# W_O's first row loaded by 16 transfers of 15, 14, ... 1 and 8 partitions

## The chip, the cores and the metric

The kernel runs on one core of a Trainium2 chip. The metric is the device time of one execution in microseconds; times of several executions are given as a median. One core has five engines with instruction streams of their own: TensorE (PE in the profile, with its weight loads as PEld), VectorE (DVE), ScalarE (ACT), GpSimd (POOL) and SyncE (SP), which here only issues transfers and waits. Its 16 DMA engines move the bytes; a transfer that is issued is cut over several of them, and they work through what is queued in order.

## The reference, cut to what matters

One decode step of a parallel block: attention over the last 4096 cached positions and a gated feed-forward layer, both fed from the same normalised input, and both added to it.

```python
xn = layernorm(x)                                  # x: 4 x 1 x 512
q = (xn @ wq) as 32 heads of 128
k, v = last 4096 positions of k_cache, v_cache     # 8 heads of keys and values
o = softmax(q k^T / sqrt(128)) v                   # 4 query heads share one of keys and values
attn = o @ wo                                      # wo: 4096 x 512
ffn = (silu(xn @ w_gate) * (xn @ w_up)) @ w_down
out = x + attn + ffn
```

All tensors are bf16. The four sequences, eight key-value heads, 4096 positions and 128 columns make 64 MiB of K and V in all; the weights are another 13 MiB, of which W_O is 4 MiB.

## The kernel before

The order of everything is written out by hand, one stream per engine, with semaphores between them. All transfers of weights, K and V are issued by SyncE, in one order: W_Q, W_gate, W_up, then for each of the eight key-value heads K in two halves and V (with W_down behind the first V), then W_O, then half of the output. K and V have one buffer each. A half of K for the next head is issued when TensorE has transposed that half of the head before (`load_k` waits on `s_tr`), V when the head before has gone through its second product (`load_v` waits on `s_pv`). W_O has a buffer of its own, and its loads wait for nothing but their turn behind the last V.

A head's loop on TensorE (L487 to L506): 16 chunks of K are transposed into PSUM (L414), copied out by VectorE and ScalarE (L330, L283), and multiplied with the queries (L427). The maxima are reduced and fed back (L434, L439), ScalarE takes the exponentials (L286), and the product with V is accumulated along with the denominators (L450, L455). Matmuls whose result nobody reads (`spin`, L467) stand in some of the waits.

After the last head comes the tail. TensorE multiplies the gated activations with W_down (L473, 14 matmuls), finishes the last head's sums (L462, L463) and permutes the attention output (L513); VectorE scales it (L353 to L358) and puts it into `OP` (L374). Then W_O: its 4096 rows are held as `WO`, 128 partitions by `NR` = 32 rows of 512 columns, so that partition p holds rows 32p to 32p + 31. In the text, a row of W_O is one of these 32: 1 KB on each of 128 partitions, 128 KB in all. The rows come in four loads, cut at `WOS`:

```python
WOS = (0, 22, 27, 30, 32)
def load_wo(n, a, b):
    eng.dma_start(WO[:, a:b, :], wo_ap[:, a:b, :]).then_inc(d_wo[n], 16)
```

For each load q TensorE waits on `d_wo[q]` and then multiplies its rows (L517 to L528). Rows 0 to 21 go four at a time into one PSUM tile (`acc4`, L473). When they are done, ScalarE copies this tile to `S2` (L294). Rows 22 to 26 go straight into the output's tile (`acc`, L477, four matmuls for each row); then TensorE waits for the copy, sums its four parts with a selection matrix (L477 with `sel4` and `S2`), and takes rows 27 to 29 and 30 to 31. VectorE adds x (L377), and SyncE and ScalarE store the output in four transfers (L268, L297).

Of the kernel before, what the change touches and what calls it, by code (L numbers as in the profile page):

```python
# [10 lines left out]
def bass_parallel_sum__sliding_block_cached__swiglu_ffn__decode_kernel(  # L11
# [10 lines left out]
    out: bass.AP,  # L22
):
    B, _, D = A_x.shape
    _, HKV, Sk, Dh = A_k_cache.shape
    HQ = A_wq.shape[1] // Dh
    F = B_w_gate.shape[1]
# [18 lines left out]
    OFF = -1.0e9  # L46
    WOS = (0, 22, 27, 30, 32)
    WOE = 22
    NR = HQ * Dh // 128

    def sb(name, shape, dtype, align=32):
        return nc.alloc_sbuf_tensor(name, shape, dtype, align_bytes=align)
# [5 lines left out]
    WD = sb("wd_sb", [128, NF, D], BF16, 512)  # L58
    WO = sb("wo_sb", [128, NR, D], BF16, 512)
    X = sb("x_sb", [B, D], BF16, 512)  # L60
# [24 lines left out]

    OP = sb("oP", [128, NR, 32], BF16)
    X4 = sb("x4", [128, D // 4], BF16)
# [12 lines left out]
    dq = sb("dq", [128, 4], FP32)  # L100
    dr = sb("dr", [128, NR], BF16)
    sel = sb("sel", [128, 32], FP32)
# [20 lines left out]
    acc4_ps = ps_S[1]  # L123
    perm_ps = ps_kt[2][:, 0:B * NR]

    def sem(name):
        return nc.alloc_semaphore(name=name)
# [7 lines left out]
    d_wo = [sem("d_wo%d" % q) for q in range(4)]  # L135
    d_k = [sem("d_k%d" % s) for s in range(2)]
    d_v = sem("d_v")
    s_const = sem("s_const")
    s_zero = sem("s_zero")
    s_var = sem("s_var")  # L140
# [34 lines left out]
    wd_ap = B_w_down.rearrange("(p t) n -> p t n", t=NF)  # L175
    wo_ap = A_wo.rearrange("(p r) n -> p r n", r=NR)

    def kv_ap(cache, g, a, b):
        return cache[:, g, Sk - W:, :].rearrange("b (j t) d -> j b t d", j=NJ)[:, :, a:b, :]

    with nc.Block() as block:

        @block.gpsimd
        def _(eng):
# [19 lines left out]
            def select(t, pattern, op, fill, base, mult):  # L204
                eng.affine_select(t, t, pattern=pattern, compare_op=op, fill=fill, base=base,
                                  channel_multiplier=mult)
# [9 lines left out]
            select(dq[:], [[-32, 4]], ALU.is_ge, 0.0, 0, 1)  # L216
            select(dr[:], [[-1, NR]], ALU.not_equal, 1.0, 0, 1)
            eng.drain()
# [19 lines left out]
        @block.sync  # L238
        def _(eng):
            H = NT // 2  # L240

            def load_k(g, h):
                if g > 0:
                    eng.wait_ge(s_tr, NCH * (g - 1) + (h + 1) * NCH // 2)
                eng.dma_start(KB[:, h * H:(h + 1) * H, :], kv_ap(A_k_cache, g, h * H, (h + 1) * H)).then_inc(d_k[h], 16)

            def load_v(g):
                if g > 0:
                    eng.wait_ge(s_pv, g)
                eng.dma_start(VB[:], kv_ap(A_v_cache, g, 0, NT)).then_inc(d_v, 16)  # L250

            def load_wo(n, a, b):
                eng.dma_start(WO[:, a:b, :], wo_ap[:, a:b, :]).then_inc(d_wo[n], 16)

            eng.dma_start(WQ[:], wq_ap).then_inc(d_wq, 16)
            eng.dma_start(WG[:], wg_ap).then_inc(d_wg, 16)
            eng.dma_start(WU[:], wu_ap).then_inc(d_wu, 16)
            for g in range(HKV):
                load_k(g, 0)
                load_k(g, 1)  # L260
                load_v(g)
                if g == 0:
                    eng.dma_start(WD[:], wd_ap).then_inc(d_wd, 16)
            for q in range(4):
                load_wo(q, WOS[q], WOS[q + 1])
            eng.wait_ge(s_y, 1)
            for n in range(2):
                eng.dma_start(out_ap[n], y[32 * n:32 * n + B, :]).then_inc(d_out, 16)  # L268
            eng.wait_ge(d_out, 64)
# [110 lines left out]
        def _(eng):  # L380
# [91 lines left out]
            def acc4(n, left, right, start, stop):  # L472
                return mm(acc4_ps[32 * n:32 * n + 32, :], left, right, start=start, stop=stop, skip_group_check=True)  # L473

            def acc(left, right, start, stop):
                for n in range(4):
                    last = mm(acc_ps[32 * n:32 * n + B, :], left, right[:, HD * n:HD * (n + 1)],  # L477
                              start=start, stop=stop, skip_group_check=True)
                return last
# [36 lines left out]
            eng.wait_ge(s_pc, 1)  # L516
            for q in range(4):  # L517
                eng.wait_ge(d_wo[q], 16)
                for e in range(WOS[q], WOS[q + 1]):
                    if e < WOE:  # L520
                        last = acc4(e % 4, OP[:, e, :], WO[:, e, :], False, e >= WOE - 4)
                    else:
                        last = acc(OP[:, e, 0:B], WO[:, e, :], e == WOE, e == NR - 1)
                if WOS[q + 1] == WOE:
                    last.then_inc(s_e, 1)
                if q == 1:
                    eng.wait_ge(s_ec, 1)
                    acc(sel4[:], S2[:], False, False)  # L528
# [29 lines left out]
```

## Time and profile before

| | us |
|---|---|
| median of 3 runs | 196.94 (196.72 to 197.49) |
| the profiled execution | 196.62 |
| its span, first to last instruction | 194.9 |
| PE busy | 160.3 (82%) |
| DVE busy | 101.7 (52%) |
| ACT busy | 61.1 (31%) |
| HBM read | 81.01 MB, 416 GB/s over the span |

The profile is that of one execution. Its page gives busy time of each engine, a digit or a rate for each fortieth of the span, and the chain that ended last, followed back from the last instruction to what released each step. Other views give the same execution in more detail: the chain in order of time, a timeline of instructions, the issues of transfers with the time from issue to landing, the instructions of one source line, and the busy time and DMA rate in stretches that one chooses. A row of the timeline reads: start, duration, engine, line, operation, written tile <- read tiles, shape, count. The engine SPq is SyncE's queue of issues; the duration there is that of issuing, not of moving. In the row of a stretch, x counts the instructions that touch it.

### The profile page before, as it was taken

Reading aid. Unit: us, or ns where it says so; the run is one execution under the profiler, and the core shown is the slowest. Engines: PE = TensorE matmul, PEld = TensorE weight load, DVE = VectorE, ACT = ScalarE, POOL = GpSimd, SP = SyncE. Lnnn points to the kernel's source line nnn. Section 1 sums busy time; section 2 is a strip of 40 time slices with the busy share of each in tenths; the row PEclk is TensorE's granted clock in tenths of the full one; section 3 lists DMA queues with packets and bytes.
Section 4 is the critical chain, followed back from the end, with each engine's and each line's share of the span. In section 5 each row is a group of like instructions: output and inputs, shape, how many; then the busy total and the mean of one; then the engine's idle time right before and its main releaser. Section 6 shows DMA issues by size and latency. Waiting matters only on the chain.

```text
span 194.9 us, 8285 instructions
## 1 busy us (share of the span) xinstructions
PE 160.3 (82%) x3646; PEld 131.6 (68%) x3646; DVE 101.7 (52%) x217; ACT 61.1 (31%) x77; POOL 12.0 (6%) x51
## 2 busy tenths in 40 slices
PE   0137759958699979997999799979997999799984
PEld 0127759946698569856985597559756976697632
DVE  4200025870478348824882588258825882588230
ACT  2020002524064406440634063407340734073401
POOL 8870000000000000000000000000000000000000
PEclk9999999985999999999999999999999999999999
DMA  6999999999999999999999999999999999999991
GB/s 216 430 435 430 418 427 437 434 424 423 427 481 425 387 430 474 430 397 430 464 430 414 430 454 430 414 430 447 437 420 430 441 430 420 430 441 430 436 396 67
DMA packets 4688, 81.13 MB, mean 416 GB/s; under 512 B 580, under 2 KB 584, under 8 KB 968
## 3 DMA queue, kind: packets, MB, share of 16 engines
q1 hardware_dynamic: 4624, 81.01, 97.2%
q8 instruction: 6, 0.10, 0.2%
q10 hardware_dynamic: 56, 0.01, 0.0%
q14 instruction: 2, 0.02, 0.0%
HBM read 81.01 MB, written 0.00 MB: 416 GB/s over the span
## 4 chain that ended last, share of the span: by engine, by line
DMA 63%; PE 32%; DVE 2%; issue 1%; ACT 0%; SPq 0%; DVEq 0%
DMA kbuf<-in_A_k_cache_dram 52%; PE ps_kt L414 18%; DMA wu_sb<-in_B_w_up_dram 11%; PE ps_s L427 5%; PE ps_o L399 2%; PE ps_kt L467 2%; PE ps_s L473 1%; PE ps_o L463 1%; PE ps_o L450 1%; PE ps_o L462 1%; DVE kT L330 1%; PE ps_s L439 0%; PE ps_s L477 0%; DVE oP L374 0%; ACT s L294 0%
## 5 line engine op out<-in xcount | busy, mean ns | idle before, releaser
L414 PE MATMUL ps_kt<-ident,kbuf 128*128 128x128 bf16 x1024 | 76.5, 221 | 10.2 <-DMA kbuf<-in_A_k_cache_dram 8.2
L330 DVE COPY kT<-ps_kt 128x1024 bf16<-128x1024 bf16 x88 | 57.6, 686 | 21.6 <-PE ps_kt L414 21.6
L414 PEld LDWEIGHTS ps_kt<-ident,kbuf 128*128 128x128 bf16 x1024 | 59.2, 98 | 13.4 <-DMA kbuf<-in_A_k_cache_dram 13.4
L283 ACT ACTIVATE kT<-ps_kt 128x1024 bf16<-128x1024 bf16 x40 | 41.0, 1024 | 65.5 <-PE ps_kt L414 65.5
L427 PE MATMUL ps_s<-qC,kT 128*128 128x16 bf16 x1024 | 44.6, 170 | 3.1 <-DVE kT L330 2.1
L427 PEld LDWEIGHTS ps_s<-qC,kT 128*128 128x128 bf16 x1024 | 37.5, 97 | 4.6 <-DVE kT L330 4.1
L286 ACT ACTIVATE p<-ps_s 128x512 bf16<-128x512 f32 x32 | 16.5, 602 | 34.7 <-PE ps_s L439 34.7
L467 PE MATMUL ps_kt<-own,ones 128*128 128x512 bf16 x102 | 25.9, 380 | 0.0
L336 DVE TENSOR_REDUCE mx<-ps_s 128x16 f32<-128x512 f32 x32 | 22.0, 689 | 5.7 <-PE ps_s L427 3.6
L450 PEld LDWEIGHTS ps_o<-vbuf,p 128*32 128x32 bf16 x1024 | 17.8, 102 | 4.6 <-ACT p L286 4.6
L450 PE MATMUL ps_o<-vbuf,p 128*32 128x128 bf16 x1024 | 19.2, 228 | 0.3
L348 DVE COPY osb<-ps_o 128x128 f32<-128x128 f32 x8 | 2.3, 292 | 29.9 <-PE ps_o L455 29.9
L455 PE MATMUL ps_o<-p,ones 128*32 128x256 bf16 x64 | 17.0, 287 | 0.0
L467 PEld LDWEIGHTS ps_kt<-own,ones 128*128 128x128 bf16 x102 | 8.2, 98 | 8.2 <-issue 1.1
L439 PE MATMUL ps_s<-cm,own 128*128 128x512 bf16 x32 | 9.1, 411 | 1.0 <-DVE cm L345 1.0
L385 PE MATMUL ps_s<-i,xn 4*128 4x4 f32 x4 | 0.6, 261 | 9.2 <-POOLq L226 9.2
L385 PEld LDWEIGHTS ps_s<-i,xn 4*128 4x128 f32 x4 | 0.6, 206 | 9.2 <-POOLq L226 9.2
L455 PEld LDWEIGHTS ps_o<-p,ones 128*32 128x32 bf16 x64 | 6.5, 101 | 0.0
L439 PEld LDWEIGHTS ps_s<-cm,own 128*128 128x128 bf16 x32 | 2.6, 101 | 5.7 <-DVE cm L345 3.5
L392 PE MATMUL ps_s<-xnT,wq_sb 128*128 128x4 bf16 x128 | 3.6, 166 | 3.4 <-DMA wq_sb<-in_A_wq_dram 3.4
L392 PEld LDWEIGHTS ps_s<-xnT,wq_sb 128*128 128x128 bf16 x128 | 3.5, 104 | 3.5 <-issue 3.5
L362 DVE TENSOR_SCALAR ex<-ex 128x56 f32<-128x56 f32 x1 | 0.2, 192 | 9.1 <-ACT ex L290 9.1
(84 smaller groups left out, 77.4 us busy)
## 6 DMA issues: line engine op xcount, KB each, us to landing
kbuf<-in_A_k_cache_dram SPq DMA_DIRECT2D x16, 2048.0 KB, 14.1
vbuf<-in_A_v_cache_dram SPq DMA_DIRECT2D x8, 4096.0 KB, 16.5
wq_sb<-in_A_wq_dram SPq DMA_DIRECT2D x1, 4096.0 KB, 12.3
wo_sb<-in_A_wo_dram SPq DMA_DIRECT2D x1, 2816.0 KB, 22.6
wg_sb<-in_B_w_gate_dram SPq DMA_DIRECT2D x1, 1792.0 KB, 16.7
wu_sb<-in_B_w_up_dram SPq DMA_DIRECT2D x1, 1792.0 KB, 20.9
wd_sb<-in_B_w_down_dram SPq DMA_DIRECT2D x1, 1792.0 KB, 42.1
wo_sb<-in_A_wo_dram SPq DMA_DIRECT2D x1, 640.0 KB, 23.5
```

The lines of the kernel that those rows point to most:

```text
L283: eng.activation(KT[:, c % 4], kt_ps[c % 3], ACT.Copy).then_inc(s_ea, 1)
L286: eng.activation(P[:, BT * q:BT * (q + 1), :], ps_S[q][:].rearrange("p (t n) -> p t n", n=NH), ACT.Exp, scale=SCALE).then_inc(s_p, 1)
L330: eng.tensor_copy(KT[:, c % 4], kt_ps[c % 3]).then_inc(s_ev, 1)
L336: eng.tensor_reduce(mx[:, q, :], ps_S[q][:].rearrange("p (t n) -> p n t", n=NH), AX.X, ALU.max)
L392: last = mm(q_ps[:, h * B:(h + 1) * B], WQ[:, c, h * Dh:(h + 1) * Dh], XnT[:, c, :], start=(c == 0 and h == 0), stop=(c == NC - 1), skip_g ...
L399: last = mm(o[:, t * B:(t + 1) * B], w[:].rearrange("p c (m t) -> p c t m", t=NF)[:, c, t, :], XnT[:, c, :], start=(w is WG and t == 0 and ...
L414: last = eng.transpose(kt_ps[c % 3][:, k, :], KB[:, CH * c + k, :], ident[:])
L427: last = mm(ps_S[q][:, NH * t:NH * (t + 1)], KT[:, c % 4, k, :], QC[:], start=(t == 0), stop=False, skip_group_check=True)
L439: mm(ps_S[q][:].rearrange("p (t n) -> p t n", n=NH), own[:], CM[:].unsqueeze(1).to_broadcast([128, BT, NH]), start=False, stop=True, skip_ ...
L450: mm(O_ps[32 * n:32 * n + 32, :], P[:, t:t + 2, :].rearrange("p t n -> p (t n)"), VB[:, t, :], start=(t < 4), stop=(t >= NT - 4), skip_gro ...
L455: last = mm(den_ps[32 * n:32 * n + 32, :], ones[:, 0:32], P[:, DT * e:DT * (e + 1), :].rearrange("p t n -> p (t n)"), start=False, stop=(e ...
L467: mm(ps_kt[k][:], ones[:], own[:].unsqueeze(1).to_broadcast([128, 4, 128]), skip_group_check=True)
```

## The change

The first of W_O's 32 rows is taken out of the first load. It is loaded by 16 transfers of its own, issued ahead of the other W_O loads, each over a run of neighbouring partitions: the first over 15 partitions (0 to 14), the next over 14 (15 to 28), and so on down to one partition (119), and a last one over eight (120 to 127). All 16 count on one new semaphore, `d_w1`. The first load of W_O then covers rows 1 to 21. TensorE, ahead of its first matmul on W_O, waits for the first load as before and in addition for the 16 small ones. The bytes, the matmuls and the other loads are the same.

```diff
@@ -46,6 +46,7 @@
     WOE = 22
+    WO1 = [n for n in range(15, 0, -1)] + [8]
     NR = HQ * Dh // 128
@@ -135,6 +136,7 @@
     d_v = sem("d_v")
+    d_w1 = sem("d_w1")
@@ -261,7 +263,13 @@
-            for q in range(4):
+
+            p = 0
+            for n in WO1:
+                eng.dma_start(WO[p:p + n, 0:1, :], wo_ap[p:p + n, 0:1, :]).then_inc(d_w1, 16)
+                p += n
+            load_wo(0, 1, WOS[1])
+            for q in range(1, 4):
                 load_wo(q, WOS[q], WOS[q + 1])
             eng.wait_ge(s_y, 1)
@@ -516,6 +524,8 @@
                 eng.wait_ge(d_wo[q], 16)
+                if q == 0:
+                    eng.wait_ge(d_w1, 16 * len(WO1))
                 for e in range(WOS[q], WOS[q + 1]):
```

## The prediction

> **What bounds the kernel now.** I read the page first: its span, the DMA slices and the chain that ended last.
>
> ```profile
> span 194.9 us, 8285 instructions
> ...
> DMA  6999999999999999999999999999999999999991
> GB/s 216 430 435 430 418 427 437 434 424 423 427 481 425 387 430 474 430 397 430 464 430 414 430 454 430 414 430 447 437 420 430 441 430 420 430 441 430 436 396 67
> ...
> DMA 63%; PE 32%; DVE 2%; issue 1%; ACT 0%; SPq 0%; DVEq 0%
> ```
>
> The 16 DMA engines are busy from the first slice to the last but one, and 63% of the chain that ended last (the last row) is transfers: the 81 MB set the pace of the loop over heads. W_O is the last thing in the queue, so the change can only touch the end. There I read the chain of waits in order of time.
>
> ```profile
> 153.55 14.13 DMA kbuf<-in_A_k_cache_dram
> ...
> 188.74 0.73 DVE oP L374
> 189.46 0.04 issue
> 189.51 1.49 PE ps_s L473 x22
> 191.00 0.02 issue
> 191.02 0.61 ACT s L294
> 191.67 0.74 PE ps_s L477 x28
> 192.44 0.29 DVE y_sb L377
> ```
>
> The last DMA in it is a K load that ends at 167.7. No piece of the last 3.7 us is one: the attention output (L374), 22 matmuls on W_O's first load (L473), ScalarE's copy, the last 28 matmuls (L477), the sum. The next question is how close behind this chain the four W_O loads land. The view of DMA issues gives the time from issue to landing, SyncE's timeline the issue.
>
> ```profile
> vbuf<-in_A_v_cache_dram SPq DMA_DIRECT2D x8, 4096.0 KB, 16.5
> wo_sb<-in_A_wo_dram SPq DMA_DIRECT2D x1, 2816.0 KB, 22.6
> wo_sb<-in_A_wo_dram SPq DMA_DIRECT2D x1, 640.0 KB, 23.5
> wo_sb<-in_A_wo_dram SPq DMA_DIRECT2D x1, 384.0 KB, 24.0
> wo_sb<-in_A_wo_dram SPq DMA_DIRECT2D x1, 256.0 KB, 24.2
> x<-in_A_x_dram ACTq DMA_DIRECT2D x4, 1.0 KB
> ```
>
> ```profile
> 165.71 0.54 SPq L250 DMA_DIRECT2D vbuf<-in_A_v_cache_dram  x1
> 166.29 2.02 SPq L253 DMA_DIRECT2D wo_sb<-in_A_wo_dram  x4
> 192.75 0.67 SPq L268 DMA_DIRECT2D out_dram<-y_sb  x2
> ```
>
> The first load lands at 166.29 + 22.6 = 188.9, 0.6 us before its matmuls at 189.51. The second, issued about 0.6 us after the first, lands at about 190.4; the third, half a microsecond behind, at about 191.4; the last, issued some 0.43 us before the end of the group at 168.31, at 167.9 + 24.2 = 192.1. When are the last three used?
>
> ```profile
> 190.49 0.57 PEld L477 LDWEIGHTS ps_s<-wo_sb,oP 128*4 128x4 bf16 x20
> 191.78 0.42 PEld L477 LDWEIGHTS ps_s<-wo_sb,oP 128*4 128x4 bf16 x20
> ```
>
> The same line cut into stretches:
>
> ```profile
> core 0: us, PE busy (x) PEld busy (x), PEclk, DMA share, GB/s
> 191.78:191.97 0.19, 0.19 (x16) 0.19 (x13) 1.00 0.00 0
> 191.97:192.05 0.08, 0.08 (x16) 0.08 (x8) 1.00 0.00 0
> 192.05:192.09 0.04, 0.04 (x16) 0.00 (x1) 1.00 0.00 0
> 192.09:192.21 0.12, 0.12 (x20) 0.10 (x8) 1.00 0.00 0
> ```
>
> The second load has 0.1 us to spare, the third 0.4. The last 20 matmuls are 12 on the third load and 8 on the fourth, and the stretches of L477 show the weight loads stop between 192.05 and 192.09 and the last eight go after 192.09, when the fourth load has just landed. So the last landing is already on the path, but by 0.04 to 0.08 us only. That is the whole that an earlier W_O can bring; a later one costs its full amount.
>
> **The change part by part.** *The tail it aims at.* The DMA view of the stretch 185 to 193 us has slices of 0.2 us; beside it is the rate of the steady loop.
>
> ```profile
> GB/s 338 451 788 113 451 225 901 225 451 225 353 205 568 481 282 282 358 410 379 420 410 410 410 399 399 369 297 189 200 174 123 123 82 102 0 0 0 0 0 0
> ```
>
> ```profile
> core 0: us, PE busy (x) PEld busy (x) DVE busy (x) ACT busy (x) POOL busy (x), PEclk, DMA share, GB/s
> 60.00:100.00 40.00, 37.14 (x868) 30.34 (x865) 24.96 (x52) 15.14 (x19) 0.00 (x0) 1.00 1.01 433
> ```
>
> The rate holds about 400 to 190.0, is half of it at 190.4 and is gone at 191.8. So the engines are not level: about half end near 190.3 and the rest over the next 1.5 us. Levelling could draw the last end in, but no view numbers the engines.
>
> *The bytes per engine.* The row of W_O is 128 x 1 KB, eight rows for each of 16 engines before. If a transfer of n partitions runs on engines 0 to n-1, one row each, engine 0 gets 16 rows, engine 7 nine, engine 8 seven, engine 15 none. One engine's rate is 433/16 = 27.1 GB/s, 38 ns for 1 KB. The slices from 188.4 to 190.0, where rows are 3 and 5 KB, average 405 GB/s, 25.3 an engine: 162 ns instead of 151 for 4 KB, so some 11 ns fixed for each row, and 49 ns for a row of 1 KB alone. Engine 0: 16 x 49 - 8 x 38 = +0.48 us; engine 7: 9 x 49 - 304 = +0.14; engine 8: +0.04; engine 15: -0.30. The last landing moves between -0.30 (all late engines are the highest) and +0.48 (the latest is engine 0). The gain is cut off at -0.06, the wait above. I take +0.10: with about eight engines late, a late one among the low half is likelier than not, but most of them get less than engine 0.
>
> [...] The row of the four loads of x, four partitions each, has no landing time where loads of 128 partitions have one, which fits fewer than 16 completions; it doesn't show which engines. [...]
>
> *Sixteen more issues on SyncE, ahead of the other W_O loads.* Their price is bounded by the nearest rows, the loads of W_O and the four-partition transfers of SyncE and ScalarE.
>
> ```profile
> L253 SPq DMA_DIRECT2D wo_sb<-in_A_wo_dram x4: 432/432/592, 166.3 to 167.9; - x4
> L268 SPq DMA_DIRECT2D out_dram<-y_sb x2: 276/312/347, 192.8 to 193.1; - x2
> L278 ACTq DMA_DIRECT2D x<-in_A_x_dram x4: 260/320/330, 9.2 to 10.2; - x4
> SPq L268 <- DVE y_sb L377: 24.4, 1, 24.4
> ```
>
> Between 0.26 and 0.59 us each, so 4.2 to 9.5 us; I take 0.35 with the gap between two, 5.6 us, since the small transfers are nearest. The rest of W_O's first load then goes out at 171.9 (170.5 to 175.8), the last load by 173.9 (at most 177.8). The queue is full that long: the last V lands at 165.71 + 16.5 = 182.2, and 4096 KB at 433 GB/s take 9.7 us, so its packets run from 172.5, on the first engines to about 180.6. SyncE has nothing else to do: it waits 24.4 us for L377. Cost nothing; without this cover it would be the whole 5.6 us. It shows only if an issue takes over (180.6 - 166.3)/16 = 0.89 us.
>
> *One more wait on TensorE*, for the 16 small loads, between the wait on the first W_O load and the 22 matmuls. The small loads are ahead of that load in the queue and land some 6 us before it, so it never holds; its instruction costs 0 to 0.04 us (the whole "issue" piece before L473, which has two waits already). I take 0.02. Behind it are all the W_O matmuls, and ScalarE's copy waits for them. Nothing else moves: K, V and the other weights are issued before.
>
> *Sum:* +0.10 + 0.02 = +0.12 us, with ends -0.06 and +0.52. The profiled execution took 196.62 us (span 194.9, 1.7 around it); the median of the runs is 196.94, 0.32 more. 196.62 + 0.12 + 0.32 = 197.06.
>
> **The rivals.** *Crowding (slower).* [...] If neighbours share a way in, the 128 KB run below 433 GB/s. At a quarter (108 GB/s) they take 1.21 us instead of 0.30 and every later load is 0.91 us late; at one engine's 27 GB/s, 4.8 us, 4.5 late. The fourth load is on the path, so all of it counts. It decides from about 1.3 us for the 16 loads (+1.0, 0.5%): 197.9 to 198.5, and 201.5 at the far end. For it: the loads are tiny and side by side. Against: the steady loop at 433 GB/s shows no such loss, and engines 1.5 us apart do not meet at the same rows. [...]
>
> *The split isn't as said.* If odd counts fall back on few engines (only 16, 8, 4, 2 or 1 of them), engine 0 gets 15 + 7 + 13 + 3 + 11 + 5 + 9 + 1 + 7 + 3 + 5 + 1 + 3 + 1 + 1 + 1 = 86 rows: 86 x 49 - 304 = +3.9 us, less 1.5 if it ends early now: 199.4 to 200.9. For it: no row shows a count that is no power of two. Against: the row of the loads of x, four partitions and no landing, fits a count that follows the rows; no row speaks for one engine.
>
> *Issues that are dear*, over 0.89 us each, leave the engines without work: at 1.1 us, (1.1 - 0.89) x 16 = +3.4 us, 200.4. All rows of issues speak against it.
>
> *The tail leaves the path:* all late engines are high; the chain of TensorE, ScalarE and VectorE sets the end: -0.06, 196.9. Nothing in the profile lets it go under that, since no DMA is in the chain after the K load.
>
> **How the numbers follow.** Forecast with the tail case in it (196.9 to 197.5): 0.66. Crowding 0.19, of which 0.05 stay under 0.5%. Split 0.05, issues 0.04, all slower. Faster by more than 0.5% has no mechanism here; 0.06 for what I do not see. So faster 0.06, same 0.71, slower 0.23; 0.5%, 1.0 us, is about what a measurement of this kernel can tell from no change. The time is that of the forecast, 197.1. The range takes the forecast with the runs' own scatter of half a microsecond downwards, 196.4, and upwards crowding to 198.3, which leaves about 0.14 above and 0.05 below.
>
> **What would show it.** Right: SyncE issues 16 small loads after 166.29 in 4 to 10 us; the fading of the rate after 190 is shorter or longer by no more than half a microsecond; L473 starts near 189.5 and L377 near 192.4 to 192.9, each counted from the first K transposes of the last head. Crowding: slices of low rate near 181 to 183 and L473 with a DMA before it in the chain. Split: one long thin tail of low rate and L477 waiting microseconds. Dear issues: SyncE still issuing after 181. Wrong altogether: a span under 194, or a time over 198.3 with none of these.

## The result, and the profile after

The changed kernel takes 198.22 us in the median of 10 runs (197.74 to 200.22), the kernel before 196.90 in 10 runs beside it: a ratio of 1.0075 (95% interval 1.0049 to 1.0102), 1.3 us slower. The profiled execution has a span of 196.8 us and took 198.55. A second series, beside an experiment below, gave 1.0054 (1.0037 to 1.0071).

First the issues of W_O's four large loads, with KB and time to landing, and SyncE's timeline, both of the kernel after.

```profile
wo_sb<-in_A_wo_dram SPq DMA_DIRECT2D x1, 2688.0 KB, 18.7
wo_sb<-in_A_wo_dram SPq DMA_DIRECT2D x1, 640.0 KB, 19.9
wo_sb<-in_A_wo_dram SPq DMA_DIRECT2D x1, 384.0 KB, 20.3
wo_sb<-in_A_wo_dram SPq DMA_DIRECT2D x1, 256.0 KB, 20.4
```

```profile
166.28 5.88 SPq L269 DMA_DIRECT2D wo_sb<-in_A_wo_dram  x16
172.20 1.78 SPq L255 DMA_DIRECT2D wo_sb<-in_A_wo_dram  x4
```

The 16 small loads are issued in 5.9 us, and the four others are out by 173.98, long before the last V has landed. But the first large load lands at 172.2 + 18.7 = 190.9 instead of 188.9, and the last, issued at 173.56, at 194.0 instead of 192.1. The timeline of the tail shows what this does (start, duration, engine, line, and in brackets the idle time before and what ended it; L481 and L485 are L473 and L477 of the kernel before):

```profile
188.73 0.72 DVE L382 CAST oP<-ps_kt 128x128 bf16<-128x128 f32 x1 [0.36 <-PE ps_kt L521]
191.02 1.47 PE L481 MATMUL ps_s<-wo_sb,oP 128*32 128x512 bf16 x22 [1.88 <-issue]
192.50 0.45 PE L485 MATMUL ps_s<-wo_sb,oP 128*4 128x128 bf16 x20
192.53 0.60 ACT L302 ACTIVATE s<-ps_s 128x512 f32<-128x512 f32 x1 [8.39 <-PE ps_s L481]
193.18 0.40 PE L485 MATMUL ps_s<-s,sel 128*4 128x128 f32 x8 [0.23 <-ACT s L302]
193.42 0.34 PE L485 MATMUL ps_s<-wo_sb,oP 128*4 128x128 bf16 x12
194.04 0.28 PE L485 MATMUL ps_s<-wo_sb,oP 128*4 128x128 bf16 x8 [0.28 <-DMA wo_sb<-in_A_wo_dram]
194.37 0.29 DVE L385 TENSOR_TENSOR y_sb<-ps_s,x 128x128 bf16<-128x128 f32 x1 [4.92 <-PE ps_s L485]
```

The attention output is ready at the same time as before (188.73 against 188.74). The 22 matmuls of L481 start 1.5 us later, as soon as the first large load is there, and the last eight of L485 wait for the last load. Everything up to W_O is unchanged; the whole loss is W_O arriving late. "issue" as the releaser of L481 hides a transfer: TensorE had nothing else to wait for.

Where did the transfers lose it? Stretches of the tail, with the mean DMA share and the rate in the last two columns, before and after:

```profile
181.00:184.00 3.00, 2.96 (x92) 1.78 (x94) 0.50 (x2) 1.93 (x4) 0.00 (x0) 1.00 0.99 428
185.00:190.00 5.00, 4.17 (x43) 1.66 (x46) 2.00 (x6) 0.00 (x0) 0.00 (x0) 1.00 0.95 397
```

```profile
181.00:184.00 3.00, 2.90 (x91) 1.72 (x93) 0.49 (x2) 1.93 (x4) 0.00 (x0) 1.00 1.05 348
184.00:185.00 1.00, 1.00 (x70) 0.84 (x59) 0.00 (x0) 0.14 (x1) 0.00 (x0) 1.00 0.83 344
185.00:190.00 5.00, 3.68 (x31) 1.39 (x30) 1.99 (x6) 0.00 (x0) 0.00 (x0) 1.00 0.94 362
```

The engines are as busy as before and move a fifth less from 181 to 184 us: the DMA share is 1.05 against 0.99 and the rate 348 GB/s against 428, so packets take longer and the queue doesn't run dry. The trace's single packets say the same. A packet of the large load (21 KB, one partition) takes 799 ns on an engine that nothing disturbs, and up to 1615 here; of the 128 small rows 114 take 46 ns, and the last starts at 182.3. Summed over the engines, the packets of 21 KB take 11.0 us too long up to 184.9 us and 5.8 us after it, when no small row is left.

### The profile page after: what moved, and what is told of

Its sections match the earlier page's. It is cut to its first block, busy times and chain, and to the rows that moved or that the text cites. A ratio compares the mean times of both kernels' runs of the same rounds, so it can differ in the third digit from the quotient of the medians.

```text
span 196.8 us, 8301 instructions
## 1 busy us (share of the span) xinstructions
PE 160.5 (82%) x3646; PEld 131.2 (67%) x3646; DVE 101.6 (52%) x217; ACT 61.1 (31%) x77; POOL 12.1 (6%) x51
## 4 chain that ended last, share of the span: by engine, by line
DMA 65%; PE 27%; SPq 4%; DVE 1%; issue 1%; ACT 0%; DVEq 0%
DMA kbuf<-in_A_k_cache_dram 44%; PE ps_kt L422 16%; DMA wu_sb<-in_B_w_up_dram 11%; DMA wo_sb<-in_A_wo_dram 10%; PE ps_s L435 4%; SPq L269 3%; PE ps_o L407 2%; PE ps_kt L475 1%; PE ps_o L458 1%; PE ps_o L471 1%; PE ps_o L470 1%; DVE kT L338 1%; SPq L255 1%; PE ps_s L447 0%; SPq L252 0%
## 5 line engine op out<-in xcount | busy, mean ns | idle before, releaser
L291 ACT ACTIVATE kT<-ps_kt 128x1024 bf16<-128x1024 bf16 x40 | 41.0, 1024 | 64.4 <-PE ps_kt L422 64.4
## 6 DMA issues: line engine op xcount, KB each, us to landing
wo_sb<-in_A_wo_dram SPq DMA_DIRECT2D x1, 2688.0 KB, 18.7
```

Source lines behind the costliest of these rows:

```text
L291: eng.activation(KT[:, c % 4], kt_ps[c % 3], ACT.Copy).then_inc(s_ea, 1)
```

## The experiments

Three theories at the start. *Crowding*: rows that an engine writes into partitions of other engines hold those engines' large packets up. *Unequal load*: the engines that got more rows just end later. *Address*: the large load now starts 1 KB into W_O's rows. Two more came up on the way: *loss of step* (engines that unequal work puts out of their order get in each other's way) and *completions* (below). No view numbers the engines or says which partitions an engine writes. The choice of partitions below rests on an assumption of mine: that the engines which carry a transfer of 8 partitions, the same eight each time, write partitions 0 to 63 in the large loads and the other eight engines 64 to 127. "Own" and "across" are meant in that sense. No run shows it; what the pairs of kernels that differ in the destination alone show is that one of each pair is the slower (1.0048 against 1.0017, 1.0204 against 1.0115, 1.0058 against 1.0002). The table has all timed runs; below it, each with its edit. All ratios are against the kernel before on the same chip, with their 95% interval.

| kernel | ratio | interval |
|---|---|---|
| one_transfer | 0.9992 | 0.9977 to 1.0006 |
| sixteen_rows | 1.0039 | 1.0025 to 1.0053 |
| eights | 1.0180 | 1.0163 to 1.0197 |
| eights_apart | 1.0101 | 1.0060 to 1.0142 |
| extra_own | 1.0017 | 1.0006 to 1.0029 |
| extra_across | 1.0048 | 1.0029 to 1.0067 |
| extra_across_one | 1.0005 | 0.9995 to 1.0014 |
| own_sixteen | 1.0115 | 1.0077 to 1.0153 |
| across_sixteen | 1.0204 | 1.0178 to 1.0229 |
| ladder_last | 1.0104 | 1.0087 to 1.0121 |
| own_whole | 1.0002 | 0.9986 to 1.0018 |
| across_whole | 1.0058 | 1.0037 to 1.0079 |
| last_one | 1.0003 | 0.9992 to 1.0013 |
| ladder_spread | 1.0045 | 1.0027 to 1.0064 |
| spread_one | 1.0011 | 1.0000 to 1.0022 |
| ladder_timed (the change again) | 1.0054 | 1.0037 to 1.0071 |

And from the trace of each, the packets of its large W_O load (21 KB, or 22 KB where row 0 is in it): how many took over 1.1 times the undisturbed 799 or 836 ns, the longest, and the sum of what all took too long.

```
kernel            long   longest ns   too long, us
before               0      836         0.0
after               83     1615        16.8   (11.0 up to 184.9 us)
ladder_again        21     1589        10.4
ladder_timed        22     1595        10.9
one_transfer         0      799         0.0
sixteen_rows        28     1620         9.4
eights              76     1713        21.1   (13.7 up to 184.9 us)
eights_apart        30     1718        14.1
extra_own            8     1402         2.9
extra_across        27     1500         8.0
extra_across_one     0      836         0.0
own_sixteen         16     1728        11.6
across_sixteen      39     1935        18.9
own_whole            0      836         0.0
across_whole        33     1495        13.1
ladder_last          0      836         0.0
```

### Row 0 cut in other ways

```diff
-    WO1 = [n for n in range(15, 0, -1)] + [8]
+    WO1 = [128]       # one_transfer
+    WO1 = [16] * 8    # sixteen_rows
+    WO1 = [8] * 16    # eights
```

> [...] Crowding (rows that an engine writes into partitions of other engines hold those engines' large packets up): nothing of the loss, 0 to +0.2 us against before, and a rate near 430 GB/s from 182 to 187 us. Uneven load of the engines: +0.1 (11 ns for each of 8 more rows). Start of the large load 1 KB further on (address): the whole loss, +1.3 us, and a rate near 360.

> [...] Crowding: +0.6 to +1.3 us against before, a low rate from 181 to 184. Uneven load: +0.1, since the load is even. Address: +1.3, as with one transfer.

> [...] Uneven load: at most +0.48 (16 x 49 ns less 304 ns), no loss of rate before 189. Address: +1.3.

```diff
# eights_apart
-    WO1 = [n for n in range(15, 0, -1)] + [8]
+    WO1 = [32 * (i // 4) + i % 4 for i in range(16)]
...
-            for n in WO1:
-                eng.dma_start(WO[p:p + n, 0:1, :], wo_ap[p:p + n, 0:1, :]).then_inc(d_w1, 16)
+            for p in WO1:
+                eng.dma_start(WO[p:p + 29:4, 0:1, :], wo_ap[p:p + 29:4, 0:1, :]).then_inc(d_w1, 16)
```

> [...] Crowding: clearly less than with eight neighbours, +0.3 to +0.8 us against before. Uneven load: the same as with eight neighbours, at most +0.48. Address: +1.3, the same in all four kernels.

With one transfer nothing is lost, and no packet is long; the rate from 181 to 184 is back:

```profile
181.00:184.00 3.00, 2.96 (x89) 1.74 (x91) 0.50 (x2) 1.88 (x4) 0.00 (x0) 1.00 0.98 417
```

So the address falls: this kernel's large load starts 1 KB in, too. Unequal load falls as the whole cause: sixteen_rows has one report for each of its 128 small rows (208 packets under 512 B from 179 to 195 us, 80 of them for the last V and W_O's four large loads), so 16 for each transfer of 16 partitions: if these are 16 engines, each has eight rows, and the kernel still loses 0.8 us. Crowding has its order right (eights with its neighbouring partitions over eights_apart with every fourth one, 200.55 against 198.85 us), but eights_apart is far above what it gave (+0.3 to +0.8, measured +1.9), which should have made me suspicious earlier.

### The same rows, other partitions

To keep W_O as before, these add transfers into W_Q's buffer, which is not read any more; the source rows are the same in both kernels of a pair. Each of the eight transfers moves 1 KB to each of 8 partitions, every fourth one; extra_across_one has the first of extra_across alone.

```diff
# extra_own; extra_across writes WQ[p + 64:p + 93:4, ...]
+    EX = [0, 1, 2, 3, 32, 33, 34, 35]
...
+            for p in EX:
+                eng.dma_start(WQ[p + 0:p + 29:4, 0:1, 0:D], wo_ap[p:p + 29:4, 0:1, :]).then_inc(d_w1, 16)
```

> [...] Crowding (rows in partitions of other engines): no packet longer than its 836 ns for 22 KB, 0 to +0.4 us. Loss of step (engines that are put out of their order by unequal work get in each other's way when reading, wherever they write): packets of 1.5 us and a loss as in the next kernel, +0.8 to +1.5.

> [...] Crowding: packets of 1.5 us from 181 to 184, +0.8 to +1.9 us, clearly more than with the partitions of their own. Loss of step: the same as with the partitions of their own, within 0.3 us.

> [...] Crowding that goes with the bytes: at most an eighth of the loss with eight, 0 to +0.2 us. Loss of step set off by any disturbance: a few packets of 1.5 us and +0.3 us or more, though it moves one 81st of a MB in ten thousand.

> The changed kernel once more, for a second profile. If the rate of 360 GB/s from 185 to 190 us in the first profile belongs to the change, it is there again and L481 waits some 1.5 us; if it is of that execution alone, the rate is back at 400 to 430 from 185 on, as with sixteen rows, and only the loss from 181 to 184 stays.

The destination matters: 8.0 us of long packets against 2.9, with the same bytes read in transfers of the same shape. But "own" partitions do not make it nought, and one transfer across has no effect at all (ratio 1.0005, no long packet). Neither crowding nor loss of step gives both.

extra_across_one also bears on a question that no view answers: which engines are late. Its load lands on eight engines (eight updates of its semaphore by data; which ones isn't shown), and its eight rows of 1 KB start when these are through with the last V:

```
starts, us: 180.459 180.480 180.721 180.757 181.106 181.512 181.737 181.861
last V landed on all 16 engines: 180.73 to 182.24
```

They are spread over the whole 1.5 us: the engines of the small load are not all early ones, and at least two of them (181.737 and 181.861) are among the very last. The lateness is older than the tail: in the kernel before, seven of the 16 engines are already late with a V that lands at 64.3 to 65.9 us.

The change's second profile (its one time 198.04 us) has the low rate from 181 to 184 again, and not the one from 185 to 190:

```profile
181.00:184.00 3.00, 2.92 (x88) 1.69 (x89) 0.50 (x3) 1.87 (x4) 0.00 (x0) 1.00 1.03 340
185.00:190.00 5.00, 3.73 (x33) 1.41 (x30) 1.99 (x6) 0.00 (x0) 0.00 (x0) 1.00 0.93 395
```

The third (ladder_timed, below) is like the second. The 5.8 us of long packets after 184.9 are in one of three profiles of the change; eights has them, too.

### Twice the dose, and the ladder at the end

own_sixteen and across_sixteen run the same eight transfers twice (two rows). ladder_last moves the ladder behind all other loads and lets it load row 31, with the wait on it ahead of the last four matmuls:

```diff
+            for q in range(4):
+                load_wo(q, WOS[q], WOS[q + 1])     # WOS = (0, 22, 27, 30, 31)
             p = 0
             for n in WO1:
-                eng.dma_start(WO[p:p + n, 0:1, :], wo_ap[p:p + n, 0:1, :]).then_inc(d_w1, 16)
+                eng.dma_start(WO[p:p + n, NR - 1:NR, :], wo_ap[p:p + n, NR - 1:NR, :]).then_inc(d_w1, 16)
```

> [...] Loss of step alone: +1.5 or more.

> [...] Crowding: +0.6 to +1.2 us over the kernel with partitions of their own, and at least three times its long packets. Loss of step alone: equal within 0.3 us.

> The ladder of 16 transfers moved to the end of the queue: it loads W_O's last row, behind all other W_O loads, and the wait on it stands before the last four matmuls. Engines have the same unequal rows. Crowding: the rows meet packets of 1 to 5 KB instead of 21 KB, and only for the engines that are late; less than half of the change's loss, +0.3 to +0.6 us against before. [...] If the place doesn't matter: +1.2 as with the change.

Crowding, by which no packet should be long on "own" partitions, missed the doubled dose: own_sixteen loses 2.6 us, with 16 long packets; across_sixteen is 1.5 us over it (+0.6 to +1.2), with 39 long packets (at least three times as many). All theories so far missed ladder_last: +1.9 us, more than the change itself, and not one long packet. Its stretches and its tail on TensorE show why:

```profile
191.50:192.00 0.50, 0.21 (x8) 0.21 (x12) 0.00 (x0) 0.24 (x1) 0.00 (x0) 1.00 0.38 94
192.00:192.50 0.50, 0.42 (x24) 0.23 (x14) 0.00 (x0) 0.00 (x0) 0.00 (x0) 1.00 0.00 0
192.50:193.00 0.50, 0.00 (x0) 0.00 (x0) 0.00 (x0) 0.00 (x0) 0.00 (x0) 1.00 0.00 0
193.00:193.50 0.50, 0.00 (x0) 0.00 (x0) 0.00 (x0) 0.00 (x0) 0.00 (x0) 1.00 0.00 0
```

```profile
192.01 0.41 PE L483 MATMUL ps_s<-wo_sb,oP 128*4 128x128 bf16 x16
194.10 0.23 PE L483 MATMUL ps_s<-wo_sb,oP 128*4 128x128 bf16 x4 [1.68 <-DMA wo_sb<-in_A_wo_dram]
```

No packet of W_O starts after 192.0, and TensorE waits for the small loads until 194.1. The bytes are there; the completions, the reports that a transfer has landed, are not. The trace has them as packets of four bytes on SyncE's queue: 208 from 179.5 us to the end of W_O in ladder_last, as many as the semaphores of the last V and of W_O have landings there (80 and 80 in the kernel before, with its five transfers). The last of them starts at 191.91 us and lands at 194.06, 2.15 us later; in the kernel before these are 191.72 and 192.06, 0.34 us apart. So each engine reports each of its transfers by itself (16 reports for a transfer of 128 partitions in the kernel before, 128 for the ladder's 16 transfers in the kernel after), the reports are sent in time, and then they land one at a time. In own_sixteen the last ones land in pairs, which I take for two engines:

```
184.67 184.72   184.87 184.92   185.08 185.13   185.28 185.33   185.49 185.53
```

One every 0.2 us in each series, while the rows behind them take 46 to 49 ns; the last ones of the first profile of the change are 0.2 us apart, too (184.094, 184.299, 184.504 and 184.708 us). So an engine with 16 small transfers moves its rows in 0.8 us and takes, by these numbers, 3.2 us to report them. Hence the theory of *completions*: the reports of one engine land 0.2 us apart, a few can be outstanding, and when too many are, the engine's next packet waits. It is mostly a large one that does; in eights, 12 of the 128 small rows take 129 to 225 ns as well. The dose fits: a transfer of 8 partitions has eight reports, and if the same eight engines carry all of them, then on "own" partitions eight transfers cost 2.9 / 8 = 0.36 us of long packets for each of these engines, 16 cost 11.6 / 8 = 1.45; a line through both has 0.14 us for each transfer beyond the fifth. Two points always lie on a line; what speaks for it is that 0.2 less the row's own 0.05 is 0.15, and that one transfer costs nothing.

### One completion instead of sixteen

```diff
# own_whole; across_whole writes partitions 64 to 92
+            eng.dma_start(WQ[:].rearrange("p c n -> p (c n)")[0:29:4, 0:16 * D],
+                          wo_ap[0:29:4, 0:16, :].rearrange("p r n -> p (r n)")).then_inc(d_w1, 16)
```

last_one is ladder_last with `WO1 = [128]`. ladder_spread has the change's own 16 transfers, with the large load cut into seven of three rows between them:

```diff
+    SPREAD = (1, 3, 5, 8, 10, 12, 15)
-            for n in WO1:
+            for i, n in enumerate(WO1):
                 eng.dma_start(WO[p:p + n, 0:1, :], wo_ap[p:p + n, 0:1, :]).then_inc(d_w1, 16)
                 p += n
-            load_wo(0, 1, WOS[1])
+                if i in SPREAD:
+                    r = 1 + 3 * SPREAD.index(i)
+                    load_wo(0, r, r + 3)
```

> The kernel before with one extra transfer ahead of W_O, 8 partitions of 16 KB, into a weight buffer that is no longer used: the bytes and the partitions of the 16 extra transfers to partitions of their own, in one. [...] Completions (each holds its engine some 0.2 us): no packet over 836 ns, +0.5 to +0.7 us, against +2.6 with 16 transfers. Unequal bytes put the engines out of step: long packets again, +1.5 us or more.

> [...] Completions alone: as with the partitions of their own, +0.5 to +0.7 us. [...]

> The control for the ladder at the end: W_O's last row as one transfer of 128 partitions behind all others. Completions: one for each engine, so the last landing is near 192.2 and the time +0.1 us (0 to +0.3) against before, 1.8 us less than with the ladder there. If it is the place (a transfer of 1 KB rows at the end, or the wait on it): near the ladder's +2.0.

> The change with its large load cut into seven of three rows each, and the 16 small transfers spread between them, two or three ahead of each: same small transfers, same partitions, same unequal bytes. An engine has at most four completions in the 1.0 us that a load of three rows takes. Completions: few packets of 3 KB over 121 ns, and +0.6 to +1.0 us against before, from 48 more rows at 6 to 11 ns and the unequal bytes. Partitions: long packets throughout, +1.3 us or more.

own_whole moves as many bytes as own_sixteen, to "own" partitions too, with eight reports instead of 128 (120 packets under 512 B from 179 us on, 240 in own_sixteen, 112 in the kernel before): 197.16 us against 199.47, no long packet. Unequal bytes alone put nothing out of step; they cost 0.0 us by the ratio and 0.3 by the medians, less than the 0.5 to 0.7 expected. (Its rows are of 16 KB, but small rows are not the cause either: one_transfer and last_one have rows of 1 KB and no long packet.) Not all of the 2.3 us between the two is transfers. In the profile of own_sixteen TensorE runs the 22 matmuls at half its clock (granted clock 0.50 from 192 to 194 us):

```profile
191.55 2.74 PE L477 MATMUL ps_s<-wo_sb,oP 128*32 128x512 bf16 x22 [2.42 <-issue]
```

They take 1.47 us in the kernel before. The last load of W_O lands 2.5 us later than before in own_sixteen (194.55) and 0.5 in own_whole (192.53), and the span of own_sixteen is 3.3 us longer: some 0.8 us is the clock. The same holds for the profiles of eights and across_sixteen (the 22 matmuls take 2.75 and 2.73 us); the table of packets is free of it. last_one against ladder_last: 196.88 against 198.82, with 16 reports for the row against 128 (128 against 240 packets under 512 B from 179 us on), without such a loss in either. TensorE takes the last 20 matmuls of last_one in one go:

```profile
192.11 0.47 PE L483 MATMUL ps_s<-wo_sb,oP 128*4 128x128 bf16 x20
```

That settles completions as a cause. across_whole shows that it is not the only one: eight reports again, and 13.1 us of long packets, where own_whole, with another destination alone, has none. That two engines now write the same partitions would explain it, but isn't shown. The eight rows of 16 KB themselves, 611 ns each in own_whole, take up to 1008. First own_whole, then across_whole, from 181 to 184 us:

```profile
181.00:184.00 3.00, 2.96 (x73) 1.57 (x73) 0.75 (x3) 1.62 (x4) 0.00 (x0) 1.00 1.02 438
```

```profile
181.00:184.00 3.00, 2.02 (x9) 0.61 (x8) 0.78 (x3) 1.59 (x4) 0.00 (x0) 1.00 0.85 258
```

Which of the two is the change's? ladder_spread has its partitions and its unequal bytes, with the completions spread out, and its median is 0.65 us over the kernel before, where the change's is 1.3. Its packets are not all as expected: 115 of the 1024 of 3 KB take over 1.1 times their 121 ns, up to 149. All its packets of 2 to 5 KB together take 5.9 us too long, nearly all of it after 184.9, and the profile doesn't tell crowding there from the low rate of the first profile of the change. The last two runs set its control beside the change: spread_one, the seven loads with row 0 as one transfer.

> The spread ladder's control: W_O's first row as one transfer of 128 partitions, then the same seven loads of three rows. 48 more rows for each engine than with one load, at 6 to 11 ns: +0.3 to +0.5 us against before, no packet of 3 KB over 121 ns. What the spread ladder loses beyond it, some 0.4 us, is then the unequal bytes (at most 0.48). If the control is as slow as the spread ladder, the cutting is all of its loss and the small transfers cost nothing when they are spread.

> The changed kernel, for its time beside the control on one chip and a third profile: ratio 1.006 to 1.0085, packets of 21 KB up to 1.6 us from 181 to 184 us, the rate back at 400 to 430 from 185 on (as in the second profile, not the first).

The cutting alone costs 0.3 us by the medians (197.13 against 196.83) and 0.2 by the ratio of 1.0011. So of the spread ladder's loss 0.35 us by the medians, or 0.7 by the ratios, are the small transfers: their unequal bytes and what is left of crowding, not taken apart. The profiles don't show it: in them the last load lands at 192.98 (ladder_spread) and 192.97 (spread_one). The change itself came out a little under the ratio expected of it, at 1.0054. So that both the number of transfers (own_sixteen against own_whole, 1.0115 and 1.0002) and the destination (across_whole, 1.0058) count is shown; how the change's loss is shared between them is not measured, only estimated (next section).

## Why the prediction was wrong, point by point

- *Issues on SyncE*: right. 5.6 us were forecast for 16, 5.88 measured; the last load goes out at 173.98 (173.9), behind the last V.
- *The wait on TensorE*: right that it doesn't hold. The last of the small loads' reports lands at 184.7, 6.3 us ahead of L481, though some 2 us later than assumed.
- *The split isn't as said*: no. The new semaphore is moved 144 times by transfers in the trace, once for each of 16 transfers at its issue, and 128 times as data land, as often as the transfers have partitions: that fits n engines for n partitions. Which engines these are, the lowest-numbered or others, no run shows.
- *The tail*: 0.04 to 0.08 us was all that an earlier last landing could have brought. That stands, and no kernel here is clearly faster than the one before.
- *Bytes per engine, +0.10 us (-0.06 to +0.48)*: the step that failed. A row was priced by its bytes and 11 ns, 49 ns in all, and that is what a row takes (46 ns recorded). But this was taken for the price of a *transfer*. Each small transfer also has a report on each of its engines, these land 0.2 us apart, and by the line through the two doses some five can be behind one another before the engine's next large packet waits. By the prediction's count, which no run shows engine by engine, eight engines carry 16 to 9 of the ladder's transfers. With the 0.14 us beyond 5.4 transfers from the kernels on "own" partitions, that is an estimate of 1.44 + 1.31 + ... + 0.49 = 7.7 us on these eight engines and 0.3 on the other eight, of the 10.4 to 11.0 us measured up to 184.9. The term for a transfer's completion was missing from the sum, put at nothing without a reason; I had the four-partition loads of x in hand, and looked at their issue time alone.
- *Late engines*: that a late one is likelier than not in the low half is not shown, since no run numbers the engines. What is shown is that small loads fall on late ones: at least two of the eight engines of extra_across_one's transfer are among the very last (181.74 and 181.86 us). That mattered more than I made of it. In the three profiles of the change the last landing of W_O moves by 1.3 to 1.9 us, while 10.4 to 16.8 us over 16 engines is 0.65 to 1.05 in the mean; the rest I put down to the spread between engines, which no view shows.
- *Crowding*, the rival with 0.19: it named the place, the sign and the size (+1.0 to +1.6) well, and the destination does count (across_whole, 1.0058 against 1.0002), but it was expected to slow the small rows, and in the change 114 of the 128 take 46 ns; what is slow are the large packets, up to 1615 ns instead of 799. In the change it is the smaller part by the estimate above, what completions leave of the 10.4 to 11.0 us. No run shows a way in that neighbouring partitions share, or the quarter of the rate (108 GB/s) that the rival's sum used: at that rate a row would take some 150 ns on each of 16 engines.
- *The chances*: 0.71 on "no change" rested on a list of mechanisms that had no price for the thing that the change adds most of, transfers. The time lay just inside the range, 198.22 of at most 198.3. That was luck: the range reached so far up for crowding alone, and by the estimate above a mechanism that was not on the list filled most of it.

What stays open: the low rate from 185 to 190 us in the first profile of the change and in eights, when the small rows are over. It was not there in two further profiles.

## What to carry to other kernels

Count transfers by engine, not only bytes: on a queue that is kept full, as here, one more small transfer cost each engine that it touches, by the estimates above, about 0.2 us of completion once some five were behind one another, four times what its 1 KB takes to move (46 ns). If engines are to be loaded unequally, do it with few long rows (16 KB on each of eight engines moved the last landing by 0.5 us in one transfer and by 2.5 in sixteen), find out from a pair like own_whole and across_whole which destination costs nothing (no long packet and 13.1 us of them), and from a probe like extra_across_one how late the engines of a small transfer are. And a stage whose last wait is 0.06 us has no more to give than that.

## What the runs showed of the hardware that was not expected

Reports of transfers come 0.2 us apart, with nothing else to move: the last in ladder_last land at 193.64, 193.84 and 194.04 us, and at 193.86 and 194.06, which fits two engines. The change's 16 small transfers have 128 landings by data, one for each partition of each.

In some profiles TensorE runs at half its clock around its wait for W_O, in others not. In ladder_timed it waits 1.54 us, and the clock (0.50, third column from the right) is at half for the 22 matmuls, which take 2.74 us; in the first profile of the change it waits 1.88 us and they take 1.47. In sixteen_rows they take 2.60 us behind a wait of 0.83 (clock 0.50 from 191 to 193), in eights_apart 1.47 behind one of 2.38 (clock 1.00): the length of the wait alone doesn't decide it.

```profile
190.90 2.74 PE L481 MATMUL ps_s<-wo_sb,oP 128*32 128x512 bf16 x22 [1.54 <-issue]
```

```profile
191.00:193.00 2.00, 2.00 (x21) 0.76 (x23) 0.00 (x0) 0.00 (x0) 0.00 (x0) 0.50 0.49 194
```
